# Three filler slots fewer: routed rows turned via DRAM, gate and up turned in one slot, parts of y added by GpSimd, and the tail's S^T in threes

## The chip, the cores and the metric

The kernel runs on one core of one Trainium2 chip. The metric is the device time of an execution in microseconds; three runs of the kernel before lie between 1411.35 and 1411.8 us, with a median of 1411.75. The engines are TensorE (PE, with its weight loads PEld), VectorE (DVE), ScalarE (ACT), GpSimd (POOL) and SyncE (SP, which here only issues DMAs).

## The reference

The input x has 2048 rows of 512 values. Two branches are computed from it and mixed per row:

```python
def reference(...):
    g = sigmoid((x * gate_w).sum(-1, keepdims=True))
    # branch A: softmax attention, 32 heads of 16, no mask
    q, k, v = heads(x @ wqkv)
    a = (softmax(q @ k.T * 16 ** -0.5) @ v) @ wo
    # branch B: the two rows with the largest r = x @ w_r go through a SwiGLU block
    r = x @ w_r
    idx = argsort(-r)[:2]
    y = (silu(x[idx] @ w_gate) * (x[idx] @ w_up)) @ w_down      # F = 1792
    b = x;  b[idx] += y * sigmoid(r[idx])
    return g * a + (1 - g) * b
```

## The kernel before, in words

Attention is cut into 32 units (a pair of heads times half of the queries; the last four units take two pairs and a quarter each) of 16 steps, 512 steps in all. A step takes 128 keys. For it PE computes four tiles of S^T (128 keys by 512 queries, `s_piece`, L675), ScalarE takes the exponential of each into a tile of P (L677, or L687 for a double tile), and PE multiplies P with V into the bank `av` (`av_mm`, L698, four concurrent matmuls, eight instructions). Three tiles of P exist. The row maxima that the exponential needs come first: `m_piece` (L594) computes scores in the other orientation, VectorE reduces them (L598) out of the banks `mxa` (two banks, one double tile) and `mxb`, and `m_unit` and `m_rows` (L646 to L666) split a unit's maxima into high and low halves on GpSimd and send them through SP into rows 48 and 49 of Qx. The maxima run 21 steps ahead of S^T.

After a lead the main loop runs in rounds of three steps. The order of one round is written out by hand in `ORDER`: s is one S^T tile, m one max piece, A the P V of one step (two steps late), f one slot for filler work. A round has 12 s, 12 m, 3 A and 1 f. There are 2048 max pieces, 84 of them done in the lead, so the loop ends after 164 rounds, at step 492. The generator `slots` says what fills the f of each round, in this order: projections of the head groups 1, 2 and 3 (`proj`, L155, 32 slots a group, three matmuls in each); a slot between group 1 and group 2 in which the two routed rows are turned on PE (`x_rows`, L383); gate, its transposes, up, its transposes, two empty slots, down (`ff_in` L404, `ff_t` L418, `ff_down` L442); a slot that adds the four parts of y with a matmul (`ff_sum`, L451); and the output products with wo (`wo_part`, `wo_last`, L513). All of them write the one bank `fl`. What a slot leaves to be evicted stands in the list `late` and is issued at the start of the next round.

Work that belongs to a step rather than a slot is put in with `at_step` and issued when that step ends. Pieces for VectorE in the gaps between reductions wait in `gaps`. All DMAs of SP stand in one queue in program order; so does GpSimd's work: evictions and splits of projections, the scaling of the residual rows by 1 - g (`acc_scale`, L474), the addition of products (`acc_add`, L480).

After the 164 rounds there is a second loop for the last 20 steps, in which no maxima are left. It issues two pairs of S^T (`s_pair`: the banks cycle through st and st, st and mxb, the double mxa), then the P V of two steps before, and in every second step one filler slot. In the last 21 steps the output product is finished by VectorE straight out of its bank (`finish`, L564) and stored. The last P V are followed by `tail`, which normalises the last unit, multiplies it with wo and stores the last rows.

At the end of unit 30 (step 495) VectorE copies the bank `av` to SBUF (`av_out`, L707); the bank `av` is the only one for P V.

Of the kernel before, what the change touches and what calls it, by code (L numbers as in the profile page):

```python
# [36 lines left out]
def gated_mix(ctx: ExitStack, tc: tile.TileContext, xT, x, wqkv, wo, w_rg, w_gate, w_up, w_down,  # L37
# [58 lines left out]
    idx2 = cp.tile([2, 1], U32, name="idx2")  # L96
    Mr = cp.tile([128, 3 * EL], F32, name="Mr")
    rsel = cp.tile([2, 1], F32, name="rsel")
    xsel = cp.tile([2, D], F32, name="xsel")
# [4 lines left out]
    x_scr = dram.tile([S, D], F32, name="x_scr")  # L104
    i_scr = dram.tile([128, 1], U32, name="i_scr")
    r_scr = dram.tile([4 * 128, 128], F32, name="r_scr")
    l_scr = [dram.tile([128, 16], F32, name=f"l_scr{i}") for i in range(3)]
# [39 lines left out]
    def proj(g, which, nb, piece):  # L147
        i = "qk".index(which)
        wh, wl = W[g]
        ps = fl_tile() if g else st_tile()  # L150
        n = 0
        for terms in (((wh, xh), (wl, xh)), ((wh, xl),)):
            for c in range(4):
                for a, b in terms:
                    nc.tensor.matmul(ps, a[:, i, c, :], b[nb][:, c, :], start=n == 0, stop=n == 11)  # L155
                    n += 1
                    if n % piece == 0 and n < 12:
                        yield
        if g:
            if (g, which, nb) == (2, "q", 3):  # L160
                late.append((split_w, (3, (1,))))
                at_step(now[0] + 2, split_w, 3, (0,))
            late.append((evict, (g, which, nb, ps)))
            yield
            return
        ev = ev0(which, nb)
        scale = 0.25 if which == "q" else 1.0
        split(ev[:, 0], ev[:, 1], ps, scale=scale)
        first_rows(which, nb, ev)
        scr.append((0, which, nb, ev))  # L170
# [197 lines left out]
    def gather():  # L368
        nc.gpsimd.indirect_dma_start(out=xsel, out_offset=None, in_=x,
                                     in_offset=bass.IndirectOffsetOnAxis(ap=idx2[:, :1], axis=0))  # L370
        nc.gpsimd.memset(xselT, 0.0)

    def route_gate(i):
        if i == 0:
# [3 lines left out]
            nc.vector.reciprocal(rsel, rsel)  # L378

    def x_rows():  # L380
        ps = fl_tile((128, 4, 2))
        for c in range(4):
            nc.tensor.transpose(ps[:, c, :], xsel[:, c * 128:c * 128 + 128], ident[:2, :2])  # L383
        late.append((nc.scalar.activation, (xselT[:, :, 0:2], ps, AF.Copy)))


    ff = {}
# [22 lines left out]

    def ff_evict(name, shape, ps):
        ff[name] = o_tile(name, shape)
        nc.scalar.activation(ff[name], ps, AF.Copy)

    def ff_t(i, name):
        ps = fl_tile((FK, 4, 128))
        for cc in range(4):
            nc.tensor.transpose(ps[:, cc, :], ff[name][:, cc * FK:(cc + 1) * FK], ident)  # L418
        late.append((ff_gu, (i, ps)))

    def ff_gu(i, ps):
        if i == 0:
            ff["gu"] = o_tile("gu", [FK, 2, 4, 4, 2])
        nc.scalar.activation(ff["gu"][:, i], ps.rearrange("p c (j m) -> p c j m", m=32)[:, :, :, 0:2], AF.Copy)

    def ff_act():
        ff["e"] = o_tile("ffe", [FK, 4, 4, 2])
# [10 lines left out]
    def ff_down():  # L438
        ps = fl_tile()
        for cc in range(4):  # L440
            for j in range(4):
                nc.tensor.matmul(ps[32 * j:32 * j + 32, :], ff["hT"][:, cc, j, :], ff["down"][j][:, cc, :],  # L442
                                 start=cc == 0, stop=cc == 3)
            if cc < 3:
                yield
        late.append((ff_evict, ("y4", [128, D], ps)))
        yield

    def ff_sum():
        ps = fl_tile((2, 512))  # L450
        nc.tensor.matmul(ps, sel_j, ff["y4"], start=True, stop=True)  # L451
        late.append((ff_out, (ps,)))

    def ff_out(ps):
        y = o_tile("ffy", [2, D])
        nc.scalar.activation(y, ps, AF.Copy, scale=rsel[:, 0:1])
        nc.gpsimd.tensor_add(y, y, xsel)
        nc.gpsimd.indirect_dma_start(out=x_scr, out_offset=bass.IndirectOffsetOnAxis(ap=idx2[:, :1], axis=0),
                                     in_=y, in_offset=None)

    def copy_x(i):
        nc.sync.dma_start(x_scr[i * 512:i * 512 + 512, :], x[i * 512:i * 512 + 512, :])


    acc = []

    def load_acc(nb):
        t = xp.tile([128, 4, D], F32, tag=f"xh{nb}", name=f"acc{nb}")
# [7 lines left out]
    def acc_add(t, ps, scale):  # L476
        a = acc[t // 4][:, t % 4, :]
        w = o_tile("w", [128, D])
        nc.scalar.activation(w, ps, AF.Copy, scale=scale[:, t:t + 1])  # L479
        nc.gpsimd.tensor_add(a, a, w)  # L480

    wop = []

# [85 lines left out]
    def wo_last(t, k):  # L569
        half, tt = divmod(t, 8)  # L570
        ah, al = lastp[half]
        ps = fl_tile()
        wo_terms(ps, ah[:k], al[:k], 3, slice(tt * 128, tt * 128 + 128), True, True)
        if now[0] < STEPS - LEAD - 1:
            late.append((acc_add, (t, ps, gg)))
        else:
            finish(t, ps)
        if k == 128:
            store(t)


# [295 lines left out]
    at_step(27, gaps.append, partial(route_gate, 1))  # L877
    at_step(20, route_index)
    at_step(26, gather)
    at_step(-8, load_w, 1)  # L880
    at_step(-5, split_w, 1)
    at_step(2, load_w, 2)
# [11 lines left out]
    def slots():  # L894
        for w, nb in order:
            yield from proj(1, w, nb, 3)
        late.append((split_w, (2,)))
        at_step(now[0] + 4, load_w, 3)
        x_rows()
        yield  # L900
        for w, nb in order:
            yield from proj(2, w, nb, 3)
        for n, (w, nb) in enumerate(order):
            yield from proj(3, w, nb, 3)
            if w == "q":
                for i in range(4):
                    at_step(now[0] + i + 1, load_ff, ("gate", "up")[i // 2], (w_gate, w_up)[i // 2],
                            ("xh", "xl")[i // 2], nb, i % 2)
        yield from ff_in("gate")
        for j in range(4):  # L910
            at_step(now[0] + 2 * j, load_down, j)
        ff_t(0, "gate")
        yield
        yield from ff_in("up")
        ff_t(1, "up")
        late.append((ff_act, ()))
        at_step(now[0] + 3, gaps.append, ff_h)
        at_step(now[0] + 3, load_wo)
        for c in range(4):
            at_step(now[0] + 6 + c, split_wo, c)  # L920
        at_step(now[0] + 5, load_at, 0, (0, 1))
        at_step(now[0] + 13, split_at, 0, (0, 1))
        yield
        yield
        yield from ff_down()
        ff_sum()
        last_tiles()
        s = now[0]
        for nb in range(4):
            at_step(s + 3 + 3 * nb, load_acc, nb)  # L930
        for t in range(16):
            at_step(s + 6 + t, acc_scale, t)
        yield
        yield from wo_groups((0, 1), (2,))
        assert now[0] > 3 * 8 * KT + 16
        yield from wo_groups((2,))
        for t in range(12, 16):
            wo_last(t, 64)
            yield
        for t in range(9):  # L940
            if t % 4 == 0:
                yield from wait((478, 494, 505)[t // 4])
            wo_last(t, 128)
            yield
# [7 lines left out]
    def p_v(s):  # L952
# [7 lines left out]
        if u % 8 == 7 and u < 24:  # L960
            for i in range(8):
                at_step(s + 6 + i, gaps.append, partial(l_out, u // 8, i))
        elif u == QU - 1:
            for i in range(8):
                at_step(s + 6 + i, gaps.append, partial(l_out, 3, i))
            for i in range(4):
                at_step(s + 16 + 2 * i, l_last, i // 2, i % 2)
                at_step(s + 19 + 2 * i, n_last, i // 2, i % 2)
            at_step(s + 27, split_last, 3)
        elif QU <= u < UNITS - 1:  # L970
            at_step(s + 3, l_unit, u, 0)
            at_step(s + 6, l_unit, u, 1)
            at_step(s + (13 if u == QU else 7), split_last, u - QU)
# [38 lines left out]
    while count["m"] < UNITS * EL:  # L1012
# [3 lines left out]
        for o in ORDER:  # L1016
# [17 lines left out]
                    run_late()  # L1034
            else:
                next(fills, None)
    for s in range(count["s"] // 4, STEPS + 2):
        run_late()
        if s < STEPS:
            start_step(s)  # L1040
            s_pair(s, 0)
            s_pair(s, 1)
        p_v(s - 2)
        if s < STEPS and (s - count["s"] // 4) % 2 == 0:
            next(fills, None)
        end_step(s)
    end_step(STEPS + 2)
    assert next(parts, 0) == 0 and not gaps and not fill and next(fills, 0) == 0, fill
    tail()

# [33 lines left out]
```

## Time and profile before

The profiled execution took 1410.94 us, its span is 1409.2 us.

| engine | busy us | share of the span | instructions |
|---|---|---|---|
| PE | 1402.5 | 100% | 9109 |
| PEld | 628.4 | 45% | 9109 |
| DVE | 1289.3 | 91% | 1543 |
| ACT | 1168.8 | 83% | 2262 |
| POOL | 315.9 | 22% | 334 |

A row of the timeline gives the start in us, the time that the row covers in us, the engine and line, the operation, the tile written and the tiles read, shapes, and how many instructions were merged; in brackets the idle time before it and what ended it. A row of the windows gives a stretch and its length, and then for PE, PEld, DVE, ACT and POOL the busy time with the number of instructions, the granted TensorE clock as a share of full speed, the DMA share and GB/s. A row of the list of waits gives who waited for whom, the total in us, the number of times and the longest. Busy shares are means over a lead, a main loop and a tail that have different limits. Matmuls are pipelined and their ends are modelled, so PE's share says little by itself; the distance between the starts of neighbouring rows says more.

### The profile page before, as it was taken

The page shows a single profiled execution, that of the slowest core. Times are in us where ns is not written, and L with a number is a line of the kernel's source. Part 1 is how long each engine was busy: PE and PEld are TensorE (multiplying, and loading weights), DVE is VectorE, ACT ScalarE, POOL GpSimd, SP SyncE. Part 2 cuts the span into 40 slices and gives each one's busy share as a digit, 9 for nine tenths or more (in the row PEclk, how much of TensorE's full clock was granted, in tenths as well). Part 3 has the DMA queues.
Part 4 walks back from the last instruction along what each step waited for, and adds up shares of the span by engine and source line. Part 5 has one row for each costly group of instructions (what it writes and reads, how often), then busy time and mean ns, then how long its engine had stood idle before and what let it go on. Part 6 is the DMA issues. An engine that isn't in the chain of part 4 may idle for free.

```text
span 1409.2 us, 24079 instructions
## 1 busy us (share of the span) xinstructions
PE 1402.5 (100%) x9109; PEld 628.4 (45%) x9109; DVE 1289.3 (91%) x1543; ACT 1168.8 (83%) x2262; POOL 315.9 (22%) x334
## 2 busy tenths in 40 slices
PE   9999999999999999999999999999999999999998
PEld 6754444444444444444444444434444444444433
DVE  6889999999999999999999999999999999999953
ACT  5578888888888888888888888888888888888986
POOL 3841101002000001200000100043722322224410
PEclk9999999999999999999999999999999999999999
DMA  8721201313122221312122342414312131111002
GB/s 263 276 48 41 55 30 39 84 39 77 53 68 92 70 61 49 73 39 79 59 90 61 101 99 72 108 55 121 84 46 54 32 67 30 29 31 49 16 31 102
DMA packets 54775, 101.24 MB, mean 72 GB/s; under 512 B 13168, under 2 KB 20592, under 8 KB 53028
## 3 DMA queue, kind: packets, MB, share of 16 engines
q1 hardware_dynamic: 53796, 98.62, 24.8%
q8 instruction: 72, 1.18, 0.4%
q10 hardware_dynamic: 576, 0.79, 0.2%
q0 software_dynamic: 288, 0.30, 0.1%
q14 instruction: 43, 0.35, 0.1%
HBM read 63.77 MB, written 36.96 MB: 71 GB/s over the span
## 4 chain that ended last, share of the span: by engine, by line
PE 99%; DMA 0%; DVE 0%; ACT 0%; DVEq 0%; issue 0%
PE av L698 36%; PE st L675 23%; PE mxa L594 12%; PE mxb L594 10%; PE fl L155 6%; PE fl L513 4%; PE st L301 3%; PE st L155 2%; PE fl L404 1%; PE mxa L628 0%; PE mxa L675 0%; PE fl L442 0%; DMA ws<-wqkv 0%; PE av L301 0%; PE st L628 0%; PE mxb L628 0%
## 5 line engine op out<-in xcount | busy, mean ns | idle before, releaser
L677 ACT ACTIVATE P<-st 128x512 f32<-128x512 f32 x2009 | 1054.8, 599 | 186.4 <-PE st L675 102.5
L598 DVE TENSOR_REDUCE Mr<-mxa 128x2 f32<-128x1024 f32 x655 | 796.5, 1216 | 1.4 <-PE mxa L594 1.3
L698 PE MATMUL av<-P,V 128*32 128x512 f32 x4096 | 545.6, 605 | 0.2 <-DVE o L707 0.2
L675 PE MATMUL st<-Qx,Kx 50*128 50x512 f32 x2009 | 530.7, 443 | 0.2 <-ACT P L677 0.2
L598 DVE TENSOR_REDUCE Mr<-mxb 128x1 f32<-128x512 f32 x654 | 451.3, 690 | 59.3 <-PE st L675 17.3
L675 PEld LDWEIGHTS st<-Qx,Kx 50*128 50x128 f32 x2009 | 277.1, 184 | 226.9 <-ACT P L677 208.7
L594 PE MATMUL mxb<-Kx,Qx 48*128 48x512 f32 x654 | 325.1, 497 | 0.0
L594 PE MATMUL mxa<-Kx,Qx 48*128 48x512 f32 x1310 | 293.5, 417 | 0.0
L594 PEld LDWEIGHTS mxb<-Kx,Qx 48*128 48x128 f32 x654 | 119.5, 183 | 273.6 <-DVE Mr L598 272.5
L698 PEld LDWEIGHTS av<-P,V 128*32 128x32 f32 x4096 | 81.1, 108 | 141.7 <-issue 135.0
L594 PEld LDWEIGHTS mxa<-Kx,Qx 48*128 48x128 f32 x1310 | 123.1, 183 | 44.4 <-DVE Mr L598 2.3
L208 POOL TENSOR_SCALAR ev<-pe 128x512 fp32r<-128x512 f32 x24 | 35.8, 1492 | 411.3 <-ACT pe L206 411.3
L480 POOL TENSOR_TENSOR acc<-acc,w 128x512 f32<-128x512 f32 x35 | 44.8, 1281 | 202.8 <-ACT w L479 202.8
L77 POOL TENSOR_SCALAR hl<-m 128x16 fp32r<-128x16 f32 x31 | 7.9, 254 | 298.0 <-DVE m L646 298.0
L155 PE MATMUL fl<-xh,wh 128*128 128x512 f32 x96 | 42.9, 447 | 0.0
L155 PE MATMUL fl<-xh,wl 128*128 128x512 f32 x96 | 40.4, 421 | 0.0
L513 PE MATMUL fl<-woh,ahl 128*128 128x512 f32 x96 | 35.1, 446 | 0.0
L564 DVE SCALAR_TENSOR_TENSOR acc<-fl,gg,acc 128x512 f32<-128x512 f32 x11 | 8.2, 747 | 28.6 <-PE fl L513 28.6
L155 PE MATMUL fl<-xl,wh 128*128 128x512 f32 x96 | 32.6, 420 | 0.0
L209 POOL TENSOR_TENSOR ev<-pe,ev 128x512 fp32r<-128x512 f32 x24 | 30.9, 1286 | 2.0
L303 ACT ACTIVATE V<-st 128x512 f32<-128x512 f32 x15 | 9.0, 600 | 24.6 <-PE st L301 24.6
L474 POOL TENSOR_SCALAR acc<-acc,omg 128x512 f32<-128x512 f32 x16 | 24.9, 1569 | 11.0 <-PE st L675 11.0
(201 smaller groups left out, 792.5 us busy)
## 6 DMA issues: line engine op xcount, KB each, us to landing
Kx<-k_scr SPq DMA_DIRECT2D x30, 384.0 KB
Qx<-q_scr SPq DMA_DIRECT2D x52, 192.0 KB
q_scr<-ev SPq DMA_DIRECT2D x15, 512.0 KB
k_scr<-ev SPq DMA_DIRECT2D x13, 512.0 KB
xn<-x SPq DMA_DIRECT2D x4, 1024.0 KB
Qx<-hr SPq DMA_DIRECT2D x256, 2.0 KB
acc<-x_scr SPq DMA_DIRECT2D x4, 1024.0 KB
q_scr<-ev SPq DMA_DIRECT2D x15, 256.0 KB
```

The lines of the kernel that those rows point to most:

```text
L155: nc.tensor.matmul(ps, a[:, i, c, :], b[nb][:, c, :], start=n == 0, stop=n == 11)
L208: nc.gpsimd.tensor_scalar(ev[:, 0], t, 1.0, None, op0=OP.mult)
L209: nc.gpsimd.tensor_sub(ev[:, 1], t, ev[:, 0].bitcast(F32))
L301: nc.tensor.matmul(ps, a[nb][:, c, sl], b[:, c, :], start=c == 0 and n == 0, stop=c == 3 and n == 2)
L474: nc.gpsimd.tensor_scalar(a, a, omg[:, t:t + 1], None, op0=OP.mult)
L480: nc.gpsimd.tensor_add(a, a, w)
L513: nc.tensor.matmul(ps, a[:, sl], b[:a.shape[0], c, :], start=first and n == 0, stop=last and n == 2)
L594: nc.tensor.matmul(dst, Qx[u % 3][64 * j:64 * j + 48, t * 128:t * 128 + 128], k_of(u, t // 4)[64 * j:64 * j + 48, c * 512:c * 512 + 512], ...
L598: nc.vector.tensor_reduce(Mr[:, g0:g0 + (2 if r == 1 else 1)], MX[r - 1], axis=AX.X, op=OP.max, negate=True)
L675: nc.tensor.matmul(ps, k, q, start=True, stop=True)
L677: nc.scalar.activation(P[s][:, 2 * j + c, :], ps, AF.Exp)
L698: nc.tensor.matmul(AV[0][32 * ct:32 * ct + 32, :], V[:, kt, h * VW:h * VW + 32], P[s][:, ct, :], start=kt == 0, stop=kt == KT - 1)
```

## The change

- `x_rows` no longer uses PE and a slot. It is issued at step 36: SP stores the two gathered rows to DRAM, reads each back turned into `xselT` (128 partitions, four elements of 4 bytes each, two DMAs), and copies the routing weight into four places of a new tile `rsel4` (four small DMAs).
- The split of the weights of group 2 stands where that of group 3 stood already: its k half in the late work after the last projection of the group before, its q half two steps on.
- `ff_t` turns gate and up in one slot, with eight ordinary matmuls against eight columns of the identity; one eviction `ff_gu` takes both.
- `ff_sum` and its slot are gone. The eviction of y scales by `rsel4`; SP moves three of the four parts of y to partitions 0 and 1 (`ff_y4`), and GpSimd adds them and the routed rows (`ff_out`).
- `acc_scale` is issued every fourth step instead of every step, and `acc_add` is put off to a later step where the scaling stands behind it.
- The normalisation of head group 3 (`l_last`, `n_last`, `split_last`) is issued one to three steps earlier. `wo_last` leaves its eviction to the late work up to one step later, and stores such a tile four steps on.
- With three slots less, three of the output products move from the second loop into the main loop; seven stay.
- The second loop issues three pairs of S^T, then the P V of all steps whose S^T were complete before the last pairs (one or two steps), with a filler slot after the first P V of every second group. At step 495 and 496 the two P V stand next to each other.

```diff
@@ proj
-            if (g, which, nb) == (2, "q", 3):
-                late.append((split_w, (3, (1,))))
-                at_step(now[0] + 2, split_w, 3, (0,))
+            if g < 3 and (which, nb) == ("q", 3):
+                late.append((split_w, (g + 1, (1,))))
+                at_step(now[0] + 2, split_w, g + 1, (0,))
@@ x_rows
-        ps = fl_tile((128, 4, 2))
-        for c in range(4):
-            nc.tensor.transpose(ps[:, c, :], xsel[:, c * 128:c * 128 + 128], ident[:2, :2])
-        late.append((nc.scalar.activation, (xselT[:, :, 0:2], ps, AF.Copy)))
+        nc.sync.dma_start(xs_scr, xsel)
+        for m in range(2):
+            nc.sync.dma_start(xselT[:, :, m], ap(xs_scr, m * D, [[1, 128], [128, 4]]))
+        for j in range(4):
+            nc.sync.dma_start(rsel4[32 * j:32 * j + 2, :], rsel)
@@ ff_t
-    def ff_t(i, name):
-        ps = fl_tile((FK, 4, 128))
-        for cc in range(4):
-            nc.tensor.transpose(ps[:, cc, :], ff[name][:, cc * FK:(cc + 1) * FK], ident)
-        late.append((ff_gu, (i, ps)))
+    def ff_t():
+        ps = fl_tile((FK, 2, 4, 8))
+        rows = ident.rearrange("p (j m) -> p j m", m=32)[:, :, 0:2]
+        for i, name in enumerate(("gate", "up")):
+            for cc in range(4):
+                nc.tensor.matmul(ps[:, i, cc], ff[name][:, cc * FK:(cc + 1) * FK], rows, start=True, stop=True)
+        late.append((ff_gu, (ps,)))
@@ ff_sum, ff_out
-    def ff_sum():
-        ps = fl_tile((2, 512))
-        nc.tensor.matmul(ps, sel_j, ff["y4"], start=True, stop=True)
-        late.append((ff_out, (ps,)))
+    def ff_y4(ps):
+        ff_evict("y4", [128, D], ps)
+        yy = ring.tile([128, 2, D], F32, tag="w", name="yy", bufs=3)
+        ff["yy"] = yy[0:2, 0], yy[0:2, 1], o_tile("y3", [128, D])[0:2]
+        for j, t in enumerate(ff["yy"]):
+            nc.sync.dma_start(t, ff["y4"][32 * j + 32:32 * j + 34, :])
+    def ff_out():
+        y = ff["y4"]
+        for t in ff["yy"]:
+            nc.gpsimd.tensor_add(y[0:2], y[0:2], t)
+        nc.gpsimd.tensor_add(y[0:2], y[0:2], xsel)
...
@@ acc_add
-        nc.gpsimd.tensor_add(a, a, w)
+        if scaled.get(t, 0) > now[0]:
+            at_step(scaled[t], nc.gpsimd.tensor_add, a, a, w)
+        else:
+            nc.gpsimd.tensor_add(a, a, w)
@@ wo_last
-        if now[0] < STEPS - LEAD - 1:
+        if now[0] < STEPS - LEAD:
             late.append((acc_add, (t, ps, gg)))
+            if k == 128:
+                at_step(now[0] + 4, store, t)
@@ slots
-        late.append((split_w, (2,)))
-        x_rows()
-        yield
...
-        ff_t(0, "gate")
-        yield
         yield from ff_in("up")
-        ff_t(1, "up")
+        ff_t()
...
-        ff_sum()
+        ff_out()
         for t in range(16):
-            at_step(s + 6 + t, acc_scale, t)
-        yield
+            scaled[t] = s + 7 + 4 * t
+            at_step(scaled[t] - 1, acc_scale, t)
@@ p_v, unit 27
-                at_step(s + 16 + 2 * i, l_last, i // 2, i % 2)
-                at_step(s + 19 + 2 * i, n_last, i // 2, i % 2)
-            at_step(s + 27, split_last, 3)
+                at_step(s + 15 + 2 * i, l_last, i // 2, i % 2)
+                at_step(s + 17 + 2 * i, n_last, i // 2, i % 2)
+            at_step(s + 24, split_last, 3)
@@ the second loop
-    for s in range(count["s"] // 4, STEPS + 2):
-        run_late()
-        if s < STEPS:
-            start_step(s)
-            s_pair(s, 0)
-            s_pair(s, 1)
-        p_v(s - 2)
-        if s < STEPS and (s - count["s"] // 4) % 2 == 0:
-            next(fills, None)
-        end_step(s)
-    end_step(STEPS + 2)
+    first, done = count["s"] // 2, count["A"]
+    for k, p in enumerate(range(first, 2 * STEPS, 3)):
+        run_late()
+        for i in range(p, min(p + 3, 2 * STEPS)):
+            s, c = divmod(i, 2)
+            if c == 0:
+                start_step(s)
+            s_pair(s, c)
+            if c:
+                end_step(s)
+        ready = (p + 1) // 2
+        for s in range(done, ready):
+            p_v(s)
+            if s == done and k % 2 == 0:
+                next(fills, None)
+        done = ready
+    run_late()
+    for s in range(STEPS, STEPS + 3):
+        end_step(s)
```

More of the change, by code (lines that the diff above doesn't have):

```diff
@@ L98, in gated_mix @@
     rsel = cp.tile([2, 1], F32, name="rsel")
+    rsel4 = cp.tile([128, 1], F32, name="rsel4")
     xsel = cp.tile([2, D], F32, name="xsel")
@@ L104, in gated_mix @@
     x_scr = dram.tile([S, D], F32, name="x_scr")
+    xs_scr = dram.tile([2, D], F32, name="xs_scr")
     i_scr = dram.tile([128, 1], U32, name="i_scr")
@@ L371, in gather @@
         nc.gpsimd.memset(xselT, 0.0)
+        nc.gpsimd.memset(rsel4, 0.0)
     def route_gate(i):
@@ L412, in ff_evict, with ff_gu @@
         ff[name] = o_tile(name, shape)
-        nc.scalar.activation(ff[name], ps, AF.Copy)
-    def ff_t(i, name):
-        ps = fl_tile((FK, 4, 128))
-        for cc in range(4):
-            nc.tensor.transpose(ps[:, cc, :], ff[name][:, cc * FK:(cc + 1) * FK], ident)
-        late.append((ff_gu, (i, ps)))
[L421 to L424, printed above, removed]
+        nc.scalar.activation(ff[name], ps, AF.Copy, scale=rsel4[:, 0:1] if name == "y4" else 1.0)
+    def ff_t():
[5 more added lines that the diff above has]
+        late.append((ff_gu, (ps,)))
+    def ff_gu(ps):
+        ff["gu"] = o_tile("gu", [FK, 2, 4, 4, 2])
+        nc.scalar.activation(ff["gu"], ps.rearrange("p i c (j m) -> p i c j m", m=2), AF.Copy)
     def ff_act():
@@ L445, in ff_down @@
                 yield
-        late.append((ff_evict, ("y4", [128, D], ps)))
+        late.append((ff_y4, (ps,)))
         yield
-    def ff_sum():
-        ps = fl_tile((2, 512))
-        nc.tensor.matmul(ps, sel_j, ff["y4"], start=True, stop=True)
-        late.append((ff_out, (ps,)))
[L454 to L457, printed above, removed]
+    def ff_y4(ps):
[9 more added lines that the diff above has]
+        nc.gpsimd.tensor_add(y[0:2], y[0:2], xsel)
         nc.gpsimd.indirect_dma_start(out=x_scr, out_offset=bass.IndirectOffsetOnAxis(ap=idx2[:, :1], axis=0),
-                                     in_=y, in_offset=None)
+                                     in_=y[0:2], in_offset=None)
     def copy_x(i):
         nc.sync.dma_start(x_scr[i * 512:i * 512 + 512, :], x[i * 512:i * 512 + 512, :])
-    acc = []
+    acc, scaled = [], {}
     def load_acc(nb):
@@ L879, in gated_mix @@
     at_step(26, gather)
+    at_step(36, x_rows)
     at_step(-8, load_w, 1)
```

1 line of the change is left out of this document (removed).

## The prediction

> **What bounds the kernel now.** I read the page's head and busy shares first, then the list of waits, then the timeline of single rounds and of the last 60 us, engine by engine.
>
> ```profile
> span 1409.2 us, 24079 instructions
> PE 1402.5 (100%) x9109; PEld 628.4 (45%) x9109; DVE 1289.3 (91%) x1543; ACT 1168.8 (83%) x2262; POOL 315.9 (22%) x334
> PEld mxb L594 <- DVE Mr L598: 272.5, 325, 0.8
> ```
>
> PE at 100% is a modelled share, and the largest wait of the list is PE's weight load standing before VectorE's (DVE's) maxima. So I look at what a round of the main loop costs when its filler slot (the place that the change moves work between) holds different things.
>
> ```profile
> 863.85 0.96 PE L404 MATMUL fl<-gate,xselT 128*32 128x448 f32 x8
> 871.50 0.65 PE L418 MATMUL fl<-cst,gate 128*112 128x128 f32 x4
> 902.45 0.96 PE L404 MATMUL fl<-up,xselT 128*32 128x448 f32 x8
> 910.14 0.65 PE L418 MATMUL fl<-cst,up 128*112 128x128 f32 x4
> 925.56 1.06 PE L442 MATMUL fl<-wd,ffhT 112*32 112x512 f32 x8
> 948.82 1.06 PE L442 MATMUL fl<-wd,ffhT 112*32 112x512 f32 x8
> 956.56 1.02 PE L451 MATMUL fl<-y,cst 128*2 128x512 f32 x2
> ```
>
> One round lies between neighbours: 863.85 to 871.50 is 7.65; 902.45 to 910.14 is 7.69; 910.14 to 925.56 holds two rounds, one with an empty slot, and is 15.42 = 2 x 7.71; 948.82 to 956.56 is 7.74. A round takes 7.7 us whether its slot is full (1.0 us), half full or empty. VectorE sets it, and up to 1.0 us of PE work in the slot is free. The loop has 164 rounds whatever the slots hold (2048 max pieces, 84 in the lead, 12 a round), so three slots given back do not shorten it. They shorten what comes after it.
>
> ```profile
> 1352.86 0.73 PE L675 MATMUL st<-Qx,Kx 50*128 50x512 f32 x3
> 1358.53 0.73 PE L513 MATMUL fl<-woh,Kx 128*128 128x512 f32 x2
> 1359.42 0.73 PE L675 MATMUL st<-Qx,Kx 50*128 50x512 f32 x3
> 1360.09 1.06 PE L698 MATMUL av<-P,V 128*32 128x512 f32 x8
> 1361.08 0.50 PE L675 MATMUL mxa<-Qx,Kx 50*128 50x512 f32 x2
> 1361.75 1.07 PE L698 MATMUL av<-P,V 128*32 128x512 f32 x8
> 1362.74 0.74 PE L513 MATMUL fl<-woh,Kx 128*128 128x512 f32 x2
> 1364.31 1.07 PE L698 MATMUL av<-P,V 128*32 128x512 f32 x8
> 1365.50 0.69 DVE L707 COPY o<-av 128x512 f32<-128x512 f32 x1 [0.99 <-PE av L698]
> 1366.25 1.07 PE L698 MATMUL av<-P,V 128*32 128x512 f32 x8 [0.20 <-DVE o L707]
> 1394.17 3.05 PE L698 MATMUL av<-P,V 128*32 128x512 f32 x24
> 1352.86:1397.22 44.36, 44.16 (x291) 14.81 (x287) 9.90 (x15) 39.54 (x67) 1.28 (x1) 1.00 0.17 61
> ```
>
> These are the last 20 steps, from the first S^T to the end of the last P V (1394.17 + 3.05 = 1397.22): 44.36 us, PE busy 44.16, ScalarE (ACT) 39.54. PE's prices, from start to next start: a product with wo 0.89 (1358.53 to 1359.42), two pairs of S^T 0.67, one P V 0.99 (1360.09 to 1361.08). Two steps hold one product and take 4.21 (1358.53 to 1362.74). Check: 20 x 0.67 + 22 x 0.99 + 10 x 0.89 + 0.20 = 44.3. So the tail is PE's, with ScalarE close behind.
>
> **The change part by part.**
>
> *Three slots less.* Slots used after: 171 instead of 174. The loop keeps 164, so the tail has 7 products, not 10: 3 x 0.89 = 2.7 us off PE there. The three products that move into loop rounds cost nothing: the rows above show a full slot at 7.7.
>
> *S^T in threes.* The tail now issues three pairs, then the P V that are ready (alternately one plus a product, and two). Three pairs back to back exist in the main loop, and ScalarE's side in the tail:
>
> ```profile
> 805.06 0.73 PE L675 MATMUL st<-Qx,Kx 50*128 50x512 f32 x3
> 805.62 0.40 PE L594 MATMUL mxa<-Kx,Qx 48*128 48x512 f32 x2
> 805.95 1.07 PE L698 MATMUL av<-P,V 128*32 128x512 f32 x8
> 1353.39 1.58 ACT L677 ACTIVATE P<-st 128x512 f32<-128x512 f32 x3 [0.54 <-PE st L675]
> 1378.14 1.03 ACT L687 ACTIVATE P<-mxa 128x1024 f32<-128x1024 f32 x1
> 1379.05 1.60 ACT L677 ACTIVATE P<-st 128x512 f32<-128x512 f32 x3
> 1380.48 0.65 ACT L677 ACTIVATE P<-mxb 128x512 f32<-128x512 f32 x1
> 1350.45 0.50 PE L675 MATMUL st<-Qx,Kx 50*128 50x512 f32 x1
> 1349.81 3.04 ACT L677 ACTIVATE P<-st 128x512 f32<-128x512 f32 x6 [0.41 <-PE mxb L594]
> ```
>
> Three pairs take 0.89 (805.06 to 805.95). PE's work for two groups (three steps) is 2 x 0.89 + 3 x 0.99 + 0.89 = 5.64. ScalarE's exponentials of one group: four at 0.48 (1379.05 to 1380.48 is three) and a double one at 0.91 (1378.14 to 1379.05), 2.83; two groups 5.66. Both engines have now nearly the same load, and each bank has one group of slack, so I follow the order by hand. First S^T at 0, exponentials from 0.53 (1352.86 to 1353.39), the double one from 2.45 to 3.50. A bank is free about 0.05 after its exponential (the first of six ends near 1350.4, PE goes on at 1350.45). PE is at the next group's third pair, which needs that double bank, at 0.89 + 0.99 + 0.89 + 0.45 = 3.22: it waits until 3.55. Then two P V until 5.97, and the next third pair finds its bank free (6.38 against 6.42). So two groups take 5.97, not 5.64; before, three steps took 1.5 x 4.21 = 6.32. Gain 0.35 x 20/3 = 2.3 us. Bounds: 5.66 with no wait at all (gain 4.4), about 6.3 if every group waits 0.33 (gain about 0).
>
> *The unit's end.* P V of step 495 and of step 496, the first of the last unit, now stand next to each other, and one bank holds both sums. From P V to P V across the copy is 1366.25 - 1364.31 = 1.94, of which S^T covered 0.67; uncovered, PE waits 0.95 instead of 0.20: 0.75 lost. At the end a lone pair precedes the last two P V: its exponentials come after a whole group's and end about 0.26 after PE is ready. Tail: 2.3 - 0.75 - 0.26 = 1.3 gained.
>
> *gate and up turned at once (ff_t).* Eight ordinary fp32 matmuls with 8 columns each in one slot replace four transposes in each of two. Nearest row:
>
> ```profile
> 1397.95 1.03 PE L814 MATMUL st<-cst,o 128*128 128x4 f32 x8
> 872.08 0.49 PE L675 MATMUL st<-Qx,Kx 50*128 50x512 f32 x1
> ```
>
> Four logical fp32 matmuls with tiny columns are 8 instructions in 0.9 to 1.0, so eight are about 1.8; four transposes took 0.58 (871.50 to 872.08). A slot of 1.0 is free, so one round may grow by 0.8, or by nothing if VectorE had slack: I take 0.5. [...]
>
> *Routed rows via DRAM (x_rows), split of wq/wk, parts of y.* These must fit behind other work, on SP and GpSimd (POOL):
>
> ```profile
> 183.63 0.89 SPq L195 DMA_DIRECT2D k_scr<-ev  x2
> 201.88 5.26 SPq L666 DMA_DIRECT2D Qx<-hr  x8
> 1294.10 0.40 SPq L779 DMA_DIRECT2D l_scr<-Ls  x1
> 1298.67 0.52 SPq L781 DMA_DIRECT2D rb<-l_scr  x1
> 335.06 1.49 POOL L208 TENSOR_SCALAR ev<-pe 128x512 fp32r<-128x512 f32 x1 [10.91 <-ACT pe L206]
> 339.20 0.40 PE L383 MATMUL fl<-cst,xsel 2*128 2x2 f32 x4
> 960.24 1.27 POOL L457 TENSOR_TENSOR ffy<-ffy,xsel 2x512 f32<-2x512 f32 x1 [13.87 <-ACT ffy L456]
> ```
>
> x_rows issues seven DMAs on SP at step 36, after the store at 183.63 and ahead of the row maxima at 201.88. Store, wait for its landing (4.6 as from 1294.10 to 1298.67), two loads, four copies at about 0.6 each: some 8 us of a gap of 17; what it writes is read by the gate products, the last of whose four slots is the row at 863.85. Cost 0; with the cover gone, each us past the gap delays the unit's S^T. The split of the third weight group comes one slot earlier relative to its use: on GpSimd its first half now stands ahead of the eviction that began at 335.06 and needs about 2.8 us, PE's slot came at 339.20. Cost 0, 1.5 if it fell behind the eviction. y: three more additions of 1.27 on GpSimd plus three small DMAs, in front of the scatter; in program order the maxima's halves of that unit come before them and the next ones 40 us later. Cost 0 (up to 3.8 if something waited on them). Deferred scalings and the earlier last-group normalisation use GpSimd time that is idle (22% busy).
>
> *Sum.* -1.3 + 0.5 = -0.8. The profiled execution took 1410.94, span 1409.2; that becomes 1410.1. It was 0.8 below the median of 1411.75, so the median after is **1410.9**. A change within 0.2%, 2.8 us, is about what a measurement of this kernel cannot tell from none.
>
> **The rivals.**
> *Faster:* PE never waits for the double bank and the eight matmuls hide: 4.4 - 0.75 - 0.26 = 3.4 less, 1408.4. For it: ScalarE had 44.36 - 39.54 us idle in the tail. Against: its load per group equals PE's within 0.02. Chance 0.16.
> *Slower:* the double bank is waited for in every group. 0.33 in the other half of the 13 groups too adds only 2.1; it turns slower than before once the mean wait passes (44.36 - 41.0) / 13 = 0.26 per group, and by more than 2.8 us once it passes 0.48. At a whole double exponential less the 0.45 of the two pairs before it, 0.6, it is 4.4 up plus ff_t: 1416.5. For it: one bank pair for the third S^T. Against: the hand order lets every second group through. Chance 0.08.
> *The element-wise DMAs hold SP:* no row of this trace moves single elements; if the two loads took over 13 us more than my 0.6 each, unit 3's maxima would come late and PE would stand for the rest; 18 us over gives about 1416. Chance 0.04. [...]
> *It does nothing:* the tail is bound by ScalarE's chain already, and the moved products only open idle time on PE: 1411.8. For it: ScalarE's idle in the tail is mostly short gaps of 0.2 to 0.5. Against: PE's own work adds up to the 44.3. Chance 0.10.
>
> **How the numbers follow.** Forecast 0.62, its own range 1409.5 to 1412.5 (ff_t 0 to 0.8, tail gain 0 to 2.2). Faster by over 0.2%: the first rival, 0.16. Slower by over 0.2%: second and third, 0.12. Within: 0.72. The range reaches from the first rival, 1408.4, to 1413.2, above the forecast's own end by part of the slower cases, leaving out under 2 in 10.
>
> **What would show it.** In the profile after: rounds of 7.7 throughout, with at most one longer one, where ff_t stands; seven products in the tail; the third pair's weight load (mxa) waiting about 0.3 for ScalarE in every second group; one wait of 0.95 for DVE's copy of o; the tail 43 us from first S^T to last P V. Wrong, if any round before the tail waits for GpSimd or a DMA, or if the waits before mxa come in every group, or in none.

## The result and the profile after

The changed kernel takes 1413.64 us (median of 22 executions, 1412.26 to 1415.81), the kernel before 1411.34 (22 executions, 1410.94 to 1412.39): a ratio of 1.0015, interval 1.0009 to 1.0021. It is 2.3 us slower, where 0.8 less was forecast. The profiled execution took 1413.65 with a span of 1411.3, against 1410.94 and 1409.2. The page and the list of waits of the changed kernel:

```profile
span 1411.3 us, 24112 instructions
PE 1403.7 (99%) x9111; PEld 630.6 (45%) x9111; DVE 1287.0 (91%) x1540; ACT 1169.8 (83%) x2262; POOL 323.6 (23%) x341
PEld mxb L608 <- DVE Mr L612: 272.5, 325, 0.8
```

The wait that bounds the loop is the same to the digit, and the shares differ by one per cent at most. So the time has to be read stage by stage. The tail first, as a window from its first S^T to the end of its last P V, with two rows of PE's timeline, PE's largest new wait in it and, from ScalarE's timeline, two of its double exponentials:

```profile
1355.80:1398.97 43.17, 42.12 (x282) 14.73 (x278) 7.75 (x12) 39.55 (x68) 1.28 (x1) 1.00 0.18 62
1363.30 0.68 PE L689 MATMUL mxa<-Qx,Kx 50*128 50x512 f32 x2
1368.63 1.07 PE L712 MATMUL av<-P,V 128*32 128x512 f32 x8 [0.87 <-DVE o L721]
PEld mxa L689 <- ACT P L701: 3.5, 9, 0.5
1372.14 1.06 ACT L701 ACTIVATE P<-mxa 128x1024 f32<-128x1024 f32 x1
1395.82 1.06 ACT L701 ACTIVATE P<-mxa 128x1024 f32<-128x1024 f32 x1
```

The tail takes 43.17 instead of 44.36, as forecast. Between the two double exponentials lie eight groups, so two groups take 5.92. What else differs lies outside it. The rounds around ff_t, in PE's timeline:

```profile
888.82 0.96 PE L409 MATMUL fl<-up,xselT 128*32 128x448 f32 x8
896.53 0.95 PE L425 MATMUL fl<-cst,gate 128*112 128x8 f32 x8
897.34 0.93 PE L425 MATMUL fl<-cst,up 128*112 128x8 f32 x8
912.60 1.06 PE L448 MATMUL fl<-wd,ffhT 112*32 112x512 f32 x8
```

896.53 to 912.60 is two rounds and takes 16.07, against 15.42 in the kernel before: 0.65 more, and eight matmuls of 8 columns hold the slot for 1.74. Before the loop something is longer that the change does not touch at all. VectorE's first double reduction of the lead and its first of the main loop, in the kernel before and then in the changed one:

```profile
26.66 1.22 DVE L635 TENSOR_REDUCE Mr<-mxa 128x2 f32<-128x1024 f32 x1
86.99 1.22 DVE L598 TENSOR_REDUCE Mr<-mxa 128x2 f32<-128x1024 f32 x1 [0.77 <-PE mxa L594]
```

```profile
27.57 1.22 DVE L649 TENSOR_REDUCE Mr<-mxa 128x2 f32<-128x1024 f32 x1
88.42 1.22 DVE L612 TENSOR_REDUCE Mr<-mxa 128x2 f32<-128x1024 f32 x1 [0.76 <-PE mxa L608]
```

Between them lie 60.33 and 60.85. And behind the last instruction of VectorE and behind the span there is more as well:

```profile
1404.69 0.88 DVE L850 SCALAR_TENSOR_TENSOR acc<-mxb,gg,acc 128x256 f32<-128x256 f32 x2
```

```profile
1406.45 0.88 DVE L864 SCALAR_TENSOR_TENSOR acc<-mxb,gg,acc 128x256 f32<-128x256 f32 x2
```

From the end of these rows (1405.57 and 1407.33) to the end of the span it is 3.60 before and 3.96 after; the time outside the span (execution less span) is 1.77 before and 2.36 after (the trace's spans are 1409.17 and 1411.29).

### The profile page after: what moved, and what is told of

The parts are those of the page before. It is cut to its first block, busy times and chain, and to the rows that moved or that the text cites. A ratio compares the mean times of both kernels' runs of the same rounds, so it can differ in the third digit from the quotient of the medians.

```text
span 1411.3 us, 24112 instructions
## 1 busy us (share of the span) xinstructions
PE 1403.7 (99%) x9111; PEld 630.6 (45%) x9111; DVE 1287.0 (91%) x1540; ACT 1169.8 (83%) x2262; POOL 323.6 (23%) x341
## 4 chain that ended last, share of the span: by engine, by line
PE 95%; DMA 2%; POOL 1%; ACT 1%; issue 0%; DVE 0%; SPq 0%; DVEq 0%; ACTq 0%; POOLq 0%
PE av L712 36%; PE st L689 23%; PE mxa L608 12%; PE mxb L608 10%; PE fl L157 6%; PE fl L526 4%; PE st L303 2%; POOL p L332 1%; DMA xs<-xT 1%; DMA wvs<-wqkv 1%; PE fl L409 1%; DMA q_scr<-ev 0%; ACT P L691 0%; PE mxa L689 0%; PE fl L448 0%
## 5 line engine op out<-in xcount | busy, mean ns | idle before, releaser
L489 ACT ACTIVATE w<-fl,gg 128x512 f32<-128x512 f32 x37 | 26.2, 708 | 0.0
```

## The experiments

Each was timed in 11 executions (ff_t doubled in 6) beside the kernel before on the same chip. Its stages were read from its own profile as above: "lead" is the distance between the two reductions, "loop" goes from the first to the last double reduction of the main loop.

**1. Once more, both kernels.** Nothing is edited. First the kernel before:

> The kernel before once more. Theory 'the lead differs from execution to execution': its lead ends near 87.6 as in the four profiles taken since, 0.6 later than in the profile of before, and about 0.7 of the 2.1 between the two profiled spans is no part of the change. Rival 'the change lengthens the lead': the lead ends at 87.0 again.

Its median is 1411.14 (before beside it 1411.32), its lead ends at 86.91 and is 60.31 long. So the lead of the kernel before repeats, and the first theory fails. The changed kernel:

> The changed kernel once more, for the spread of its lead from execution to execution. 'Place of the tiles': the lead ends at 88.2 to 88.6 again and the time is 1413.6. 'Chance': the lead ends anywhere from 87.0 to 88.4.

1413.13 (before beside it 1411.80; ratio 1.0011, 1.0002 to 1.0020). The lead ends at 87.66 and is 60.88 long, the loop takes 1264.61 (before 1263.55), the tail 43.15. Where the lead starts differs between executions (26.78 here, 27.57 in the profile shown above); its length does not.

**2. The place of the tiles alone.**

```diff
@@ before.py, behind rsel
+    pad = cp.tile([128, 1], F32, name="pad")
```

> The kernel before with one unused tile of 128 x 1 beside rsel and nothing else. It moves every tile allocated behind it (xsel, xh, xl, P, the rings) up by 32 bytes per partition, from 32 past a multiple of 64 to a multiple of 64, while V, Kx and Qx stay; the change did the same with rsel4. Theory 'place of the tiles': the lead's matmuls of v_part come every 0.233 us instead of 0.227, the first reduction of the main loop begins at 88.2 to 88.5 instead of 86.99, the time is 1412.5 to 1413.5. Theory 'chance or other parts of the change': the lead ends at 86.8 to 87.3 and the time is 1411.3 as before.

The median is 1412.38 against 1411.80 (ratio 1.0006, 0.9997 to 1.0015, so by the time alone it is not told from no change), the lead 60.89 long, the loop 1263.90. The loop's first reduction begins at 87.78, which lies between the two theories, since the lead began at 26.89; its length decides. PE's groups by form between 28 and 86 us, first in the kernel before, then with the unused tile (the last numbers are busy us and the mean of one in ns):

```profile
L301 PE MATMUL st<-Kx,xl 128*128 128x512 f32 x60 | 23.5, 391 | 0.0
L301 PE MATMUL st<-wvl,xh 128*128 128x512 f32 x60 | 23.4, 389 | 0.0
```

```profile
L302 PE MATMUL st<-Kx,xl 128*128 128x512 f32 x60 | 23.9, 398 | 0.0
L302 PE MATMUL st<-wvl,xh 128*128 128x512 f32 x60 | 23.8, 396 | 0.0
```

An unused tile of four bytes a partition, and the matmuls of these two groups of 60 take 7 ns more each; from start to start their median goes from 227 to 233 ns. The matmuls of the maxima between them lie a little closer together (0.2 us in all), which leaves the lead's 0.57. The time is 0.1 below the lower end of what the first theory expected.

**3. Another 32 bytes.**

```diff
@@ after.py, behind rsel4
+    pad = cp.tile([128, 1], F32, name="pad")
```

> The changed kernel with a second unused tile of 128 x 1 behind rsel4, so that all tiles behind it lie again 32 past a multiple of 64. Theory 'place of the tiles': the lead ends near 87.0 instead of 88.42, the time falls from 1413.6 to 1411.9 to 1412.4; what then remains above my forecast is the round of ff_t and the end. Theory 'chance or other parts': lead 88.4 and 1413.6 as in the changed kernel.

1412.84, the lead 60.88 long, the loop 1264.58: as the changed kernel. So the multiple of 64, as I had put the theory, is not the point; the lead is longer at 32 bytes as well as at 64 bytes from the old place.

**4. Nothing moved.**

```diff
@@ after.py
-    rsel4 = cp.tile([128, 1], F32, name="rsel4")
@@ gather
+        ff["r4"] = ring.tile([128, 1], F32, tag="r4", name="rsel4", bufs=1)
```

> The changed kernel with rsel4 taken from the end of the last pool, so that no other tile of SBUF moves against the kernel before. Theory 'place of the tiles': the moved tiles, by 32 or by 64 bytes, cost 0.57 in the lead (from its first double reduction to the loop 60.9 instead of 60.3) and 0.4 in the loop; without the shift these are 60.3 and 1264.1, the time 1.0 below the changed kernel. Rival 'the shift is not it': 60.9 and 1264.6.

```profile
L302 PE MATMUL st<-Kx,xl 128*128 128x512 f32 x60 | 23.5, 392 | 0.0
L302 PE MATMUL st<-wvl,xh 128*128 128x512 f32 x60 | 23.4, 389 | 0.0
```

The matmuls are back at 392 and 389 ns, the lead at 60.29. Over all fourteen profiles the lead is 60.29 to 60.33 in the six with the tiles in their old places and 60.84 to 60.90 in the eight with the tiles moved. The median is 1412.23 (before beside it 1411.36), 0.87 up where the changed kernel was 1.33 up in its own comparison: 0.46 less, where the first theory has 1.0. So the lead's part is shown, and the loop's 0.4 is not: the loop took 1266.44, more than in any profile before, and not for the place of the tiles (experiment 6).

**5. ff_t in two slots.** The second half goes into the slot that stood empty.

```diff
@@ slots
-        ff_t()
+        ff_t(0, "gate")
         late.append((ff_act, ()))
...
         yield
+        ff_t(1, "up")
+        late.append((ff_mul, ()))
         yield
```

> The changed kernel with gate's four matmuls in ff_t's slot and up's four in the empty slot behind it, so no slot more. If the eight matmuls in one slot are what lengthened that round (8.34 against 7.71), both rounds are 7.7 to 7.75 and the loop is 0.6 shorter, 1264.0 instead of 1264.6. If the round was long for its other work (evictions, wo's loads), it stays at 8.2 or more. Time 0.6 below the changed kernel's 1413.1, or the same.

```profile
888.17 0.96 PE L409 MATMUL fl<-up,xselT 128*32 128x448 f32 x8
895.88 0.95 PE L424 MATMUL fl<-cst,gate 128*112 128x8 f32 x8
903.56 0.95 PE L424 MATMUL fl<-cst,up 128*112 128x8 f32 x8
911.29 1.06 PE L447 MATMUL fl<-wd,ffhT 112*32 112x512 f32 x8
```

The rounds are 7.71, 7.68 and 7.73, the loop 1264.20. The median is 1412.24 (before beside it 1411.32), and all 11 executions lie between 1411.92 and 1412.89, where the changed kernel's 11 in experiment 1 go up to 1414.57. So more hung on this slot than 0.6.

**6. What the slot does to the clock.** Two profiles happened to catch it. In experiments 4 and 8 the loop took 1266.44 and 1266.24, where the other profiles with this slot have 1264.58 to 1264.94. The windows of experiment 8 (PEclk is the third number from the right) with a row of PE's timeline there, and the window of the changed kernel in the profile shown above:

```profile
896.00:898.00 2.00, 2.00 (x19) 1.60 (x18) 1.21 (x2) 1.03 (x3) 0.00 (x0) 1.00 0.00 0
898.00:902.00 4.00, 4.00 (x24) 1.19 (x22) 2.67 (x4) 2.89 (x8) 0.52 (x2) 0.57 0.02 4
902.00:906.00 4.00, 3.83 (x30) 1.52 (x22) 3.86 (x7) 2.91 (x7) 0.48 (x2) 1.00 0.00 0
898.04 1.86 PE L712 MATMUL av<-P,V 128*32 128x512 f32 x8
```

```profile
898.00:902.00 4.00, 4.00 (x31) 1.61 (x30) 3.18 (x4) 3.17 (x8) 0.52 (x2) 1.00 0.02 4
```

Right behind ff_t the granted clock is 0.5 for 3.41 us (898.18 to 901.59 in the trace's clock record) in one and full in the other. The P V in that stretch takes 1.86 instead of 1.07, and the ten rounds around it take 79.42 instead of 78.02 (77.17 before). To see whether ff_t is the cause, it was doubled:

```diff
@@ ff_t
-        for i, name in enumerate(("gate", "up")):
+        for i, name in 2 * tuple(enumerate(("gate", "up"))):
```

> The changed kernel with ff_t's eight matmuls issued twice in their slot, 3.5 us of PE instead of 1.75; the second time writes the same again. Theory 'a stretch of such matmuls halves the granted clock for the 3.4 us behind it': with twice the stretch every execution has it, so nearly all lie at the upper group, the round is 7.7 + 0.6 + 1.75 + 1.6 = 11.7, the median 1416.5 with a mean clock of 0.998. Theory 'the halved clock comes by chance': half of the executions, the round 10.1 in the others, the median about 1415.

```profile
888.00:899.00 11.00, 11.00 (x90) 5.97 (x86) 9.59 (x11) 8.50 (x17) 0.00 (x0) 1.00 0.19 50
899.00:906.50 7.50, 7.50 (x38) 3.29 (x37) 3.69 (x4) 3.49 (x8) 0.52 (x2) 0.54 0.01 2
```

The median is 1416.93, and all six executions have a mean clock of 0.997 or 0.998. The halved stretch is here 6.83 us long, twice 3.41. The first theory holds, but for the length of the stretch and so of the round. Counted over all executions, a mean clock of 0.998 or less stands in 31 of 77 of the kernels with the eight matmuls in one slot (the changed kernel 10 of 22, and 3 of 11 in experiment 1), in 6 of 6 with sixteen, in none of 22 with four in each of two slots, in none of 94 of the kernel before and in none of the 22 of experiment 9. It also stands in 1 of the 11 of experiment 2 (1415.16 us), which has no such slot; that execution has no profile, so a halved clock seems to come from elsewhere too, seldom, and where is open. The counts may be too low, since the mean is rounded and one halved stretch takes only 0.0012 off it (half of 3.41 in 1411 us). The changed kernel's 22 executions lie accordingly: eight at 1412.3 to 1412.9, four at 1413.3 to 1413.7, the ten with 0.998 at 1413.8 to 1415.8; the medians are 1412.66 without and 1414.24 with 0.998.

The clock record also says when the stretch begins. In all three profiles that have it, the clock was full for 894.29 us before. In experiment 8 the slot's matmuls begin at 895.47 and the next work at 897.13, and the stretch begins at 898.18, 1.05 behind that. Of the six profiles with eight matmuls in one slot, two have the halved clock and four have not (both of the changed kernel and those of experiments 3 and 7); what decides between them is not shown.

**7. The tail without the threes.**

```diff
@@ the second loop, as before
-    for k, p in enumerate(range(first, 2 * STEPS, 3)):
...
+    for s in range(count["s"] // 4, STEPS + 2):
```

> The changed kernel with the second loop of before (two pairs of S^T, one P V, a product in every second step), so seven products without the threes. Theory 'the threes carry the gain': without them ScalarE's chain holds the tail where it was, 44.3 us from the first S^T to the last P V, and the time is 1.2 above the changed kernel, 1414.8. Theory 'the products alone do it': 14 steps of 2.1 with half a product each, six steps at ScalarE's four exponentials (four of 0.48 and half of 0.91, 1.89), two last P V: 43.0, the time as the changed kernel's, 1413.5.

```profile
1355.08:1398.27 43.19, 42.98 (x282) 14.02 (x278) 7.73 (x12) 39.53 (x68) 1.28 (x1) 1.00 0.18 62
```

43.19 against 43.15 to 43.17. Against the old order the threes give nothing; three products less give the whole 1.2, in either order. The median is 1414.28, higher than the 1413.5 of the second theory (6 of its 11 executions have a mean clock of 0.998, see experiment 6); its profiled execution took 1412.99, 0.39 more than the changed kernel's in experiment 1.

**8. The wait for the copy of o removed.**

```diff
@@ the second loop
-            if s == done and k % 2 == 0:
+            if s == done and (k == 3 or k % 2 == 0 and k != 4):
```

> The changed kernel with one product of the tail moved from the group behind to between the P V of steps 495 and 496, where PE waited 0.87 for the copy of the bank av. Theory 'PE sets the tail': the wait falls to 0.1 and the tail from 43.15 to 42.3 to 42.5. Theory 'ScalarE sets the tail': its chain of exponentials goes on as before, the wait turns up ahead of S^T, and the tail stays at 43.1.

```profile
1356.19:1399.31 43.12, 42.63 (x282) 15.00 (x278) 7.83 (x12) 39.53 (x68) 1.28 (x1) 1.00 0.18 63
PEld mxa L689 <- ACT P L701: 3.7, 9, 0.7
1368.04 0.73 PE L526 MATMUL fl<-woh,Kx 128*128 128x512 f32 x2
1368.98 1.07 PE L712 MATMUL av<-P,V 128*32 128x512 f32 x8
1370.57 1.57 ACT L691 ACTIVATE P<-st 128x512 f32<-128x512 f32 x3 [0.90 <-PE st L689]
```

The wait of 0.87 is gone from PE, and the tail is as long as ever, 43.12: by the numbers the second theory. But the product fills the place of the wait. It takes 0.94 (1368.04 to 1368.98), the P V behind it comes only 0.04 earlier, and ScalarE stands still for 0.90 for the next S^T, where it stood for 0.91 in the changed kernel:

```profile
1370.22 1.57 ACT L691 ACTIVATE P<-st 128x512 f32<-128x512 f32 x3 [0.91 <-PE st L689]
```

PE gains the product's old place one group later, and there it waits for ScalarE: the second mxa behind the unit's end (at 1373.60; 1373.26 in the changed kernel) begins 17.41 behind the tail's first S^T, 17.46 in the changed kernel. So the run shows that time saved on PE behind the unit's end does not shorten the tail; it does not show that ScalarE alone sets the tail. How long the tail would be without ScalarE's 0.91 was not tried. (The median, 1413.85, says little on that: 5 of the 11 executions have a mean clock of 0.998.)

**9. The end.**

```diff
@@ before.py
+    for i in range(18):
+        at_step(200 + 2 * i, nc.sync.dma_start, d_scr[i:i + 1, :], cst[0:1, 0:8])
```

> The kernel before with 18 DMAs of 32 bytes each added on SP, one in every second step from step 200, into a tensor that nobody reads; 850 DMAs instead of 832 (the change has 842). Theory 'more DMAs lengthen the end': the last one lands on another of the eight semaphores that SP waits for in turn at the end, so the stretch from VectorE's last instruction to the end of the span grows from 3.63 to 3.97, and if it is SP's longer program that is still being fetched behind the last instruction, the time outside the span grows from 1.73 to 2.35; the median rises by 0.3 to 1.0. Rival 'the end has another cause': 3.63 and 1.73, the median as before. By neither does the loop change.

```profile
span 1409.7 us, 24095 instructions
1404.88 0.88 DVE L851 SCALAR_TENSOR_TENSOR acc<-mxb,gg,acc 128x256 f32<-128x256 f32 x2
```

From VectorE's end (1405.75) to the end of the span (1409.72 in the trace) it is 3.97, as in the changed kernel, and 3.60 in the kernel before. SP's last waits, in the kernel before and then in this one, say why:

```profile
SPq L1080 <- DMA out<-acc: 2.1, 4, 0.8
SPq L1084 <- DMA out<-acc: 2.4, 2, 2.1
```

They stand in a fixed order, nine in a row. In the kernel before the last landing releases the eighth of them, here and in the changed kernel the second, and the six more behind it take 0.06 us each. The rest of the first theory fails: outside the span 1.78, not 2.35, and the median is 1411.50 against 1411.32. The same with GpSimd:

```diff
@@ before.py
+    for i in range(9):
+        at_step(200 + 2 * i, idle, i)      # a memset of 128 x 8 on GpSimd
```

> The kernel before with nine small memsets added on GpSimd, one in every second step from step 200, as many instructions as the change adds there. Theory 'GpSimd's program is still being fetched behind the last instruction': a fetch of 8 KB 2.1 us behind the span's end and 2.35 instead of 1.73 outside the span, the median 0.6 up. If it is ScalarE's program (2448 instructions instead of 2437), none of that: 1.73 and the median as before.

Outside the span 2.07, half of the way; the median 1411.43 against 1411.36. The trace's list of transfers has fetches of instructions, 8 KB each, behind the end of the span:

```
kernel                      outside the span   fetches, us behind the end of the span
before, twice               1.77, 1.77         none
one unused tile (2.)        1.77               none
18 DMAs more on SP          1.78               1.55
9 memsets more on GpSimd    2.07               1.43
changed, nothing moved      2.07               1.42
all of it mended (10.)      2.27               0.98
ff_t doubled                2.22               1.41 and 2.09
changed, product moved (8.) 2.32               1.42 and 2.09
changed, twice              2.36, 2.39         1.42 and 2.30, 1.42 and 2.11
```

No fetch, 1.77; one, 1.78 to 2.27; two, 2.22 to 2.41 (with the profiles of experiments 3, 5 and 7, which have two each). Time and fetches go together only loosely: with the 18 DMAs one fetch goes with nothing more, elsewhere with 0.3 to 0.5. Which engine's program the second belongs to was not tried.

**10. All of it mended.**

```diff
@@ x_rows, ff_evict, ff_out; ff_t as in experiment 5
-        for j in range(4):
-            nc.sync.dma_start(rsel4[32 * j:32 * j + 2, :], rsel)
+        nc.gpsimd.tensor_scalar(y[0:2], y[0:2], rsel[:, 0:1], None, op0=OP.mult)
```

> The changed kernel with gate's and up's matmuls in two slots, without rsel4 (GpSimd multiplies y by the routing weight just before the last addition, so nothing in SBUF moves and four DMAs go), and with the two loads of x_rows in halves, 840 DMAs. By the terms found so far, against the kernel before: tail -1.2, ff_t 0, shift 0, end 0, outside the span 0 to 0.6: 1410.2 to 1410.8, where before has 1411.3. Rival 'the shift was not it': 1 more, as before.

1410.90 (1410.53 to 1411.64) against 1411.36 of the kernel before: a ratio of 0.9994, 0.9985 to 1.0003. That is 0.1 above the range expected and 0.5 below the kernel before, which is not told from no change, and 1.8 below the changed kernel, each taken against the kernel before beside it. Its stages: lead 60.32, loop 1263.80, tail 43.1, end 3.62, outside the span 2.27. All was changed at once here; what each part is worth is read from the experiments before.

## Why the prediction was wrong

The step that failed is the sum, -1.3 + 0.5. Its first term held. Its second was the right size for PE's time, but left out what the slot does to the clock; and three effects were not in it at all: the place of the tiles, SP's last waits, and the time outside the span. The two profiles of experiment 1 (1411.03 and 1412.60, 1.57 apart) split so: start of the lead +0.18, lead +0.57, loop +1.06, tail -1.21, end +0.37, outside the span +0.62. The median lies higher still, since 10 of 22 executions take another 1.4 for the halved clock.

- *Tail, -1.3:* right in length (43.15 to 43.17, forecast 43.0), and for the threes in mechanism: two groups take 5.92, forecast 5.97, and the wait for the copy is 0.87, forecast 0.95. But the double bank is not waited for in every second group: PE's weight load waits for it in the third group and in each from the sixth to the thirteenth, 0.5 twice and then 0.29 and 0.42 in turn, 3.5 us in all. And the threes are not what the gain comes from. Without them the tail is 43.19: the old order with seven products is as fast. From the fifth double exponential to the thirteenth it takes 23.70 against 23.68: 6.07 for three steps where it has products and 5.62 at the end, where none are left. In the first groups ScalarE stands still four times for S^T, 2.3 us in all, the longest 0.94 and 0.91. The four groups up to the fifth double exponential (1358.26 to 1372.14) take 13.88, where the forecast's period and its 0.75 give 12.7; that the whole came out right all the same is in part luck. Neither engine sets the tail alone: 5.92 is 0.3 above PE's own 5.64 and ScalarE's 5.66.
- *Products moved, x_rows, the split and y at 0:* right. The loop's other groups of ten rounds agree within 0.2. x_rows in SP's timeline of the changed kernel:

```profile
185.21 0.89 SPq L197 DMA_DIRECT2D k_scr<-ev  x2
186.20 0.73 SPq L385 DMA_DIRECT2D xs_scr<-xsel  x1
188.70 0.92 SPq L387 DMA_DIRECT2D xselT<-xs_scr  x2
189.71 2.49 SPq L389 DMA_DIRECT2D rsel<-rsel  x4
203.45 2.61 SPq L680 DMA_DIRECT2D Qx<-hr  x4
```

  6.0 us of the gap (186.20 to 192.20), forecast 8; the two loads of single elements issue in 0.92. That rival did not come about.
- *ff_t, +0.5 with bounds 0 and 0.8:* the slot's 1.74 cost 0.65 in its two rounds, inside the bounds. But a term was missing beside it: in four executions of ten (31 of 77, by a mean clock of 0.998 or less) the clock is halved for 3.41 us behind it, 1.4 us more. The row for the price (tiny columns, eight instructions in a microsecond) was found and read for its duration only. PE was not idle ahead of the stretch: in experiment 8 it is busy 2.00 of 2.00 us from 896 to 898 (by modelled ends), with PEld at 1.60, and what ran there are the slot's weight loads and 8-column matmuls and the work behind them. That the slot brings the halved clock on fits 31 of 77 at 1.74 us, 6 of 6 with twice the matmuls and none of 22 with four in each of two slots; by what way it does so is not shown.
- *The new tile at nothing:* the step was not in the sum at all. rsel4 is four bytes a partition and costs 0.57 in the lead (experiments 2 and 4). The first ten rounds of the loop are 0.16 longer in the two profiles of experiment 1, and by 0.1 still with nothing moved, so that part is not shown. Why the same matmuls take 7 ns more with their tiles 32 or 64 bytes further stays open.
- *Ten DMAs and some instructions more, priced by the queue they wait in:* they also move the program's end, by 0.37 in the span and by about 0.6 outside it. The 0.37 is SP's last waits: with 832 transfers the last landing releases the eighth of nine, with 842 the second. Experiment 9 shows it with 850, and experiment 10 with 840 is back at 3.62. The time outside stays open: it is longer in most profiles that fetch instructions behind the end, but not in step with the number of fetches. The fetches are of 8 KB each, and the profiles do not settle what one behind the end costs.
- *The base:* 0.8 was added for the median of three runs, 1411.75; 22 executions give 1411.34. That puts the forecast 0.4 too high, in the other direction. And a change within 0.2% can be told from none here: the interval of the result is 0.06% to either side.

Of the rivals none came. The wait for the double bank comes in 9 of the 13 groups that have one, and the tail gains its 1.2 all the same; SP kept up; and "it does nothing" fails, since three products less were worth 1.2. The loss has four parts that no rival held.

## What to carry to other kernels

Matmuls with hardly any columns can cost more than their duration: here 1.74 us of them in a row brought PE's clock to a half for 3.41 us behind them in four executions of ten (31 of 77, by the mean clock), and four in each of two slots in none of 22, so split them between slots with full matmuls in between. When a change of some 0.1% is priced, what lies outside the steps counts as well: where tiles move when one is added (0.57 in the lead here), and what more transfers do to the program's last waits (0.37 here). And a new order of work is to be run against the old one with the same work: here the order got the credit in the forecast, and the work left out had earned it. Where one of PE's waits is taken away by putting other work in its place, look whether the other engine's idle time went with it, before the length of the stage is read as that engine's.

## What had not been expected

- The granted clock fell to 0.5 for 3.41 us (6.83 with twice the work) with PE busy all the time by the profile (4.00 of 4.00 us from 898 to 902 in experiment 8).
- An unused tile of 128 x 1 made two groups of 60 matmuls of the lead 7 ns slower each (391 to 398 and 389 to 396) at 32 bytes of shift, and at 64 bytes the lead is as long; with the old places they are back.
- Eighteen small DMAs in the middle of the program lengthened its last stretch from 3.60 to 3.97, and the time outside the span lies between 1.77 and 2.4 by kernel, for a reason that stays open.
